# A fused DeltaNet and MLP kernel: the order of all its steps replaced by another, and its filler products given two widths

## The chip, the cores and the metric

The kernel runs on one core of a Trainium2 chip. Its time is the device time of one execution in microseconds (us); for one core the slowest core is that core. The time before is the median of three runs.

## The reference

An attention block (DeltaNet, a recurrence with a matrix state per batch and head), then layer norm and a two-layer MLP with ReLU, added to the block's output.

```python
batch, n_heads, seq, head_dim = (4, 8, 768, 48)      # q, k, v, beta; d_model = 8 * 48 = 384
def _attn_ref(q, k, v, beta):
    k_n = k / (np.linalg.norm(k, axis=-1, keepdims=True) + 1e-06)
    state = np.zeros((B, H, D, D))
    for t in range(S):
        y[:, :, t] = einsum('bhd,bhde->bhe', q[:, :, t], state)
        v_old = einsum('bhde,bhd->bhe', state, kt)
        state = state + bt * einsum('bhd,bhe->bhde', kt, vt - v_old)
def _moe_ref(x, g_ln, w_ch1, w_ch2):                  # w_ch1 384 x 1536, w_ch2 1536 x 384, in float64
    xn = (x - mu) / np.sqrt(var + 1e-06) * g_ln
    return x + np.maximum(xn @ w_ch1, 0.0) @ w_ch2
```

## The kernel before

The sequence of 768 tokens is cut into 12 chunks of 64. For each chunk c all 32 pairs of batch and head are worked on together: 64 tokens of two batches fill the 128 partitions. All arithmetic is float32; TensorE runs each float32 matmul call as two passes, each with a weight load of its own (a transpose is one pass).

For a chunk the attention part multiplies keys with keys (`gram`, G, L819) and queries with keys (`queries`, P, L819), inverts a triangular 64 x 64 matrix for each head, and carries the state on. For chunk 0 the inverse is made by products on TensorE, E1, Z1 to E5, Z5 (`first_inverse`, L770 and L786), with transposes and masked copies on VectorE and copies on ScalarE between them. For all others `rows_inverse` (L865) stores the products to DRAM, loads them back so that each head lies in one partition, eliminates 32 x 32 blocks on VectorE (pairs of instructions at L907 and L914, each waiting for the one before), and sends the result back by DRAM; `join` (L965) puts two blocks together with two products, e and z (L981, L987; for chunk 1 also L944 and L949). `recur` (L1021) then runs ks and qs (L1033), u (L1052, L1069 or L1088), s, the update of the state (L1105), and y, the output (L1095). Each of these is 32 matmul calls on tiles of 48 or 64 rows, 64 passes.

After y comes the layer norm on VectorE and ScalarE and the turn of its result to columns: by TensorE for chunks 0 to 2 (L1183), else by a store and four loads through DRAM (`xld`, `xnj`, DMA issued by SyncE). The MLP of chunk c (`mlp`, L1388) follows: for chunk 0 L1406 and L1448, for chunks 1 and 2 L1426 and `seven` (L1502), from chunk 3 on `fifteen` (L1274) and `seven`. `fifteen` replaces 18 block products of the first layer by 15 with sums on GpSimd (`mix`, L1290), VectorE (L1330) and ScalarE (L1325, L1334); its products are L1307, each step four passes of 128 columns over a bank of PSUM. `seven` does the second layer with 7 products in place of 8 (L1523, two passes of 192 columns a step; sums on GpSimd at L1510 and L1548, on VectorE at L1541). The weights come as 64-bit words (`fetch`, L568, DMA issued by ScalarE) and are converted by ScalarE, VectorE and GpSimd (`convert`, L579).

Every operation is a step: `Line.add` (L69) notes its engine, what it reads and writes, and a number, 0 to 3031, in the order in which the program names them. A step can hold many instructions (the 32 calls of a product), and the cost and due time given to it play no part in what follows. `ORDER` (L156 to L254) is a list of these numbers, with ranges; `Line.emit` (L101) goes through it and emits each step. `in_this_order` (L25) ties each instruction to the one before it on its engine, so the list sets the order on every engine, and the order of the DMA issues across SyncE and ScalarE. An engine that waits for a step's inputs holds up everything behind it in its queue.

The list also has the letter `f` three times. There `emit` takes the bank of the next TensorE step, asserts that nothing unread lies in it, and calls `idle` (L1597), which issues a matmul of 128 columns of the identity into that bank; its result is overwritten unread.

Of the kernel before, what the change touches and what calls it, by code (L numbers as in the profile page):

```python
# [53 lines left out]
class Line:  # L54
# [46 lines left out]
    def emit(self, tc):  # L101
# [7 lines left out]
        order = []  # L109
        for w in ORDER.split():  # L110
            a, b = (0, -1) if w == "f" else map(int, (w.split("-") * 2)[:2])
            order += self.steps[a : b + 1] or [None]
        nxt = None
        for n in range(len(order) - 1, -1, -1):
            if order[n] is None:
                order[n] = nxt.out
            elif order[n].eng == "PE":
                nxt = order[n]
        live = {}
        for s in order:  # L120
            if isinstance(s, tuple):
                assert not live.get(s[:2]), s
                self.filler(s)
                continue
# [5 lines left out]
            n = len(made)  # L130
# [26 lines left out]
52-53 51 54 65 10 9 57-58 55 320 56 306 398 67 319 63 62 66 308 249 654 7 64 8 61 11-12 2 33 14 25 24 71-72 68 0 15-16 34 21 27 13  # L157
1 26 18 31 19 3 75-76 82 6 17 83 70 77 73 84 36 99 37 97 74 38 101-104 93 100 78 69 79 30 28 80 20 85-86 81 110-111 87-88 116-117
113 205 105-106 f 39 120 107-108 119 121 94 114 206-207 115 208 90 92 91 46 656 42 44 43 40 59-60 45 41 109 251 258 112 122 118
124-125 123 132 134 133 126 128 22-23 127 140 138 135 89 137 136 131 129-130 141-143 139 146 230 98 144-145 218 149 152-154 160  # L160
147-148 156 155 150 157 96 95 151 158 32 161 168 159 219 169 29 170 162-164 176 174 255 405 252 256 402 253 257 254 307 305 401
318 395 317 220 214 232 171 173 165-166 172 216 212 167 240 242 209 47 657 4 177 175 184-186 231 178 192 179-180 210 183 238 187
181-182 188-189 236 190 221 233 48 658 49-50 193-195 201 241 191 243 197 259 202 235 204 362 203 198 200 199 361 309 311 234 196 f
310 331 260-262 35 248 250 263 211 237 264-265 213 239 332 312 222 329-330 333 335 355 313 334 314-315 226 5 266-269 215 270-273
223 274-276 337 277-279 321 323 322 324-325 338 280-289 336 224 356 326 341 327 342 290-295 343 217 653 225 666 659 655 353-354
426-427 f 347 244 429 428 245 349 339 348 350 227 340 344-346 430 567 569 431 568 228 246 571 432 351 316 406 328 397 393 296 404
403 396 467 352 229 247 665 668 461 660 357 572 575 570 363 573 576 407 303 298 300 297 301 299 304 302 469 468 466 399-400 394
579 593 574 359 580 577-578 594 583 408 465 584 581 587 599 582 600 588 368 365 358 364 360 409-410 667 411 605 585 591 366 412
367 470 586 589 413 379 590 592 380 606 611 595 597 661 369 371 596 601 471-474 477 476 414 478 475 415 370 372 434 670 392 672
671 669 391 416 374 373 598 603 612 604 417 419 418 385 433 609 420-421 610 386 424 375 383 602 425 422-423 381 630-632 615-616  # L170
435-436 782-783 785 787 917 784 786 789 788 780 920 916 617 607 479-504 376 505-508 387 437 382 388 509 377 438 673 439-440 378
608 384 389 442 441 443 445 390 618-619 613 633 662 620 634 1068 1080 677 1070 1072 1074 1067 444 614 446 790 450 447-448 510-515
451 516 449 517-520 452 521-539 663 674-675 924 664 676 923 779 679-680 678 681 926 635-636 621-622 637 623-624 638-640 457 453
625-626 641 540 642 645 627 646 644 919 928 544 541 543 542 460 459 456 458 455 791 454 794 825 682 826 647 683-686 689 792 823
831 821 832 837 822 827 781 688 690 1069 845 463 1082 1073 464 1071 838 843 828 833-834 691-696 651 697-698 545-546 687 652
699-700 556 648 701-702 649 703 839 547 549 548 550-551 553 824 552 840 554-555 844 793 829 795 830 796 835 797 800 836 802 848
922 1081 846 1079 1084 851 847 852 849 557 798 930 925 628 929 927 643 931 1173 1179 1181 629 918 1183-1184 1362 921 1182 1178
704-705 1075 706-708 805-806 841 854-858 799 558-560 801 810 709 803 1172 1185 1180 861 650 859 842 561 850 1085 1083 462 862 853
1086 863 1541-1542 811 710 804 812 711-713 807 860 808 714 932-933 864-866 871 867-869 817 934 562 870 820 564 563 566 715-716 809
717-721 936 722-726 872 889 881-882 813 565 814 818 816 873-874 883-885 890 875 886 891 876 727 877 1087 815 819 935 937 892-894  # L180
938 878 880 879 939 972 1186 887-888 895 1544 1554 1556 1543 940 1076 973 907 1077 978 908-910 896-899 979 984 900 911-912 901 941
# [76 lines left out]
def kernel(  # L258
# [13 lines left out]
    nc = tc.nc  # L272
# [61 lines left out]
    ident = sb("ident", [128, 128])  # L334
# [1262 lines left out]
    def idle(key):  # L1597

        nc.tensor.matmul(banks_of[key[:2]][:, 0:128], ident, ident[:, 0:1].to_broadcast([128, 128]))
# [152 lines left out]
```

## Time and profile before

| | |
|---|---|
| median of three runs | 520.41 us (519.92 to 522.11) |
| the profiled execution: its time | 520.78 us |
| its span, first to last instruction | 519.1 us |
| mean TensorE clock in it | 0.982 |
| DMA | 54.56 MB in 181,635 packets, 105 GB/s |

The difference between the profiled execution's time and its span, 1.7 us, lies outside the instructions. How rows are read: in a timeline a row is start, duration, engine, line, operation, output and inputs, shape and how many instructions, and in brackets how long the engine was idle before it and what ended that. PE is TensorE's matmul, PEld its weight load, counted apart. DVE is VectorE, ACT ScalarE, POOL GpSimd, SP SyncE. "issue" stands for a wait that ended for no reason that the profile shows. A row of a table of windows is the stretch, its length, the busy time and instruction count of each engine (PE, PEld, DVE, ACT, POOL, unless fewer are named), the granted TensorE clock as a share of full speed, the busy share of the 16 DMA engines and GB/s. In the lists of DMA queues stand packets, MB and the share of the 16 engines' time.

### The profile page before, as it was taken

To read this page: it belongs to the slowest core of one execution; us is meant where nothing else is said; L and a number is where in the kernel's file an instruction comes from. 1 tells how busy PE (TensorE), PEld (TensorE's weight loads), DVE (VectorE), ACT (ScalarE), POOL (GpSimd) and SP (SyncE) were. 2 spreads that over 40 slices of the span, in tenths; PEclk is the share of its full clock that TensorE was granted. 3 is DMA by queue.
4 is the path that set the end of the run, shared out by engine and by line. 5 is a ranking of instruction groups with operands and counts; after the bars stand their busy time and mean duration, and the time that the engine had idled before them with its cause. 6 is when DMAs were issued, how large, how long until landed. Compare 5 with 4: busy or idle time off the path is not lost.

```text
span 519.1 us, 22785 instructions
## 1 busy us (share of the span) xinstructions
PE 487.1 (94%) x9972; PEld 448.9 (86%) x9972; DVE 360.8 (70%) x814; ACT 206.9 (40%) x462; POOL 280.3 (54%) x447
## 2 busy tenths in 40 slices
PE   5577888999899999999999999999999999999997
PEld 4466786768798889999999989999999999999996
DVE  6577739798887567988889986757988446244241
ACT  5587845423431333234242632533513514424130
POOL 3435654604554877976764274473453742564554
PEclk9878998999999999999999999999999999999999
DMA  9957876585515866345853356643404403003011
GB/s 135 294 115 204 191 154 178 107 195 95 90 26 141 156 134 109 68 88 141 167 120 55 83 108 157 132 81 66 102 10 111 104 17 93 4 1 100 2 39 30
DMA packets 181635, 54.56 MB, mean 105 GB/s; under 512 B 164888, under 2 KB 177312, under 8 KB 181536
## 3 DMA queue, kind: packets, MB, share of 16 engines
q1 hardware_dynamic: 168512, 40.10, 37.9%
q10 hardware_dynamic: 10816, 9.83, 6.6%
q0 software_dynamic: 2208, 3.17, 3.8%
q8 instruction: 78, 1.28, 1.0%
q14 instruction: 21, 0.17, 0.1%
HBM read 36.30 MB, written 16.78 MB: 102 GB/s over the span
## 4 chain that ended last, share of the span: by engine, by line
PE 79%; DMA 5%; SPq 3%; issue 3%; DVE 3%; ACT 3%; POOL 2%; ACTq 0%; DVEq 0%; POOLq 0%
PE f L1523 27%; PE f L1307 22%; PE f L1426 6%; PE f L1448 3%; SPq L410 3%; PE two L819 3%; PE by L1033 2%; PE two L1033 2%; PE by L1095 2%; DMA xnt<-xld 2%; PE two L1088 2%; PE f L1406 1%; PE two L1105 1%; DMA words<-in_moe_w_ch_dram 1%; DMA gb<-gd 1%
## 5 line engine op out<-in xcount | busy, mean ns | idle before, releaser
L1510 POOL TENSOR_TENSOR h_all<-h_all 128x256 f32<-128x256 f32 x99 | 72.7, 745 | 30.5 <-PE f L1523 13.8
L1523 PE MATMUL f<-w_sb,h_all 128*128 128x192 f32 x396 | 82.2, 331 | 1.0 <-ACT h_all L1334 0.6
L1523 PE MATMUL f<-words,h_all 128*128 128x192 f32 x396 | 76.7, 329 | 0.0
L1523 PEld LDWEIGHTS f<-w_sb,h_all 128*128 128x128 f32 x396 | 65.1, 190 | 3.0 <-ACT h_all L1334 1.6
L1330 DVE TENSOR_TENSOR h_all<-f,h_all 128x512 f32<-128x512 f32 x72 | 48.9, 685 | 26.4 <-PE f L1307 19.3
L1523 PEld LDWEIGHTS f<-words,h_all 128*128 128x128 f32 x396 | 65.0, 190 | 1.5 <-issue 0.5
L1548 POOL TENSOR_TENSOR words<-h_all 128x128 f32<-128x128 f32 x66 | 31.2, 491 | 63.4 <-ACT h_all L1334 30.4
L907 DVE TENSOR_TENSOR tmp<-xb,gb 128x31 f32<-128x31 f32 (+19 forms) x139 | 57.5, 413 | 3.9 <-POOL xb L894 0.3
L1325 ACT COPY h_all<-f 128x512 f32<-128x512 f32 x45 | 26.2, 586 | 82.4 <-PE f L1307 68.8
L914 DVE TENSOR_TENSOR xb<-xb,tmp 128x31 f32<-128x31 f32 (+19 forms) x139 | 52.6, 378 | 3.7
L410 POOL DMA_DIRECT2D tb<-in_k_dram x64 | 42.2, 662 | 0.3 <-POOL tb L1630 0.3
L1334 ACT ACTIVATE h_all<-h_all 128x512 f32<-128x512 f32 x54 | 32.7, 626 | 23.9 <-DVE h_all L1330 23.5
L1307 PE MATMUL f<-x_new,w_sb 128*128 128x128 f32 x288 | 40.3, 278 | 0.1
L1307 PE MATMUL f<-xnt,w_sb 128*128 128x128 f32 x288 | 40.2, 277 | 0.0
L1307 PEld LDWEIGHTS f<-x_new,w_sb 128*128 128x128 f32 x288 | 36.5, 191 | 0.6 <-issue 0.2
L1307 PEld LDWEIGHTS f<-xnt,w_sb 128*128 128x128 f32 x288 | 36.5, 192 | 0.6 <-issue 0.2
L1541 DVE TENSOR_TENSOR o<-f,x 128x192 f32<-128x192 f32 x33 | 11.4, 352 | 36.8 <-PE f L1523 30.9
L1426 PE MATMUL f<-xnt,w_sb 128*128 128x256 f32 x144 | 34.5, 387 | 1.4 <-issue 1.4
L1426 PEld LDWEIGHTS f<-xnt,w_sb 128*128 128x128 f32 x144 | 26.4, 190 | 5.4 <-issue 1.8
L1523 PE MATMUL f<-w_sb,words 128*128 128x192 f32 x132 | 26.3, 329 | 0.0
L682 POOL TENSOR_TENSOR v<-v,kpair 128x768 f32<-128x768 f32 x10 | 14.7, 1473 | 14.0 <-DVE pt L897 14.0
L610 POOL TENSOR_TENSOR w_sb<-words 128x768 uint32<-128x768 uint32 (+1 forms) x11 | 14.7, 1348 | 13.7 <-ACT words L600 10.2
(239 smaller groups left out, 983.4 us busy)
## 6 DMA issues: line engine op xcount, KB each, us to landing
words<-in_moe_w_ch_dram ACTq DMA_DIRECT2D x20, 384.0 KB, 4.5
gd<-gsb SPq DMA_DIRECT2D x11, 512.0 KB, 3.9
v<-in_v_dram SPq DMA_DIRECT2D x24, 192.0 KB, 4.2
kr<-in_k_dram SPq DMA_DIRECT2D x46, 96.0 KB, 3.4
out_dram<-o SPq DMA_DIRECT2D x46, 96.0 KB, 2.2
xld<-xlt SPq DMA_DIRECT2D x9, 384.0 KB, 2.4
xnt<-xld SPq DMA_DIRECT2D x36, 96.0 KB, 2.9
tb<-in_q_dram SPq DMA_DIRECT2D x40, 64.0 KB, 2.8
```

The source lines that it names most:

```text
L410: add(eng, cost, lambda: QUEUE[eng].dma_start(out=out_, in_=in_), r, w, bulk=n * ns / 16e3, np=n, **kw)
L907: lambda j=j, n=n, w=w, t=t: nc.vector.tensor_tensor(out=t, in0=xv[:, 0:n, j : j + 1].to_broadcast([128, n, w]), in1=gv[:, j : j + 1, j + ...
L914: "DVE", dve(n * w), lambda t=t, rest=rest: nc.vector.tensor_tensor(out=rest, in0=rest, in1=t, op=ALU.subtract),
L1033: nc.tensor.matmul(dst[half(e), hp, j], src[drows(hp), (e if n else key_half(c, hp, e)) * GP + j], s_all[drows(hp), e, j], start=(n == 0 o ...
L1307: nc.tensor.matmul(wide(p[:, f : f + 128]), w[:, f : f + 128], r, start=start and i == 0, stop=True, skip_group_check=True)
L1325: add("ACT", act(512), lambda: nc.scalar.copy(o, p), pk, ok)
L1330: add("DVE", dve(512), lambda: nc.vector.tensor_tensor(out=o, in0=x, in1=y, op=op), [*xk_, *yk], ok)
L1334: add("ACT", act(512), lambda: nc.scalar.activation(o, o, ACTF.Relu, scale=scale), [], ok)
L1426: nc.tensor.matmul(p[:, 0:TOK], w1_sb[:, t, f * 128 : (f + 1) * 128], xnt[:, t], start=(t == 0), stop=(t == KC - 1))
L1510: add(eng, cost, lambda: e.tensor_tensor(out=out_, in0=x, in1=y, op=op), r, w, port=2 if eng == "Pool" else 1, pr=-2)
L1523: lambda f=f, t=start and f == order[0]: nc.tensor.matmul(p[:, 0:D2], lhs(f), rhs[:, f], start=t, stop=(f == order[-1]), skip_group_check=True
L1548: lambda f=f + i: e.tensor_tensor(out=s3[f], in0=one(0, 0)[0](f), in1=one(1, 0)[0](f), op=ALU.subtract),
```

## The change

The list `ORDER` is replaced whole. It names the same 3,032 steps, each once. Of the 954 steps of TensorE, 151 stand at the same place among TensorE's steps in both lists; the stages follow each other in the same manner (inverse of chunk 0, recurrences with MLP products between them, the MLP of chunks 10 and 11 alone at the end). The words that come with the change say that the plan behind the new list lets the transfer of a TensorE block wait until other transfers have run dry; of that plan the code holds only the list.

The fillers are now two: one `f`, among the first products of chunk 0, and one `F`, ahead of step 334, the second half of y0. `F` is a matmul of 512 columns in place of 128. The new `f` stands before the product of keys of chunk 1 (step 105). In the old list the three `f` stand before the second E1 (step 122), before a turn of chunk 2's keys (step 310) and before a turn of chunk 0's layer norm (step 347).

```diff
@@ -108,19 +108,19 @@
         for w in ORDER.split():
-            a, b = (0, -1) if w == "f" else map(int, (w.split("-") * 2)[:2])
-            order += self.steps[a : b + 1] or [None]
+            a, b = (0, -1) if w in "fF" else map(int, (w.split("-") * 2)[:2])
+            order += self.steps[a : b + 1] or [w]
         nxt = None
         for n in range(len(order) - 1, -1, -1):
-            if order[n] is None:
-                order[n] = nxt.out
+            if isinstance(order[n], str):
+                order[n] = (order[n], nxt.out[:2])
             elif order[n].eng == "PE":
                 nxt = order[n]
         live = {}
         for s in order:
             if isinstance(s, tuple):
-                assert not live.get(s[:2]), s
-                self.filler(s)
+                assert not live.get(s[1]), s
+                self.filler(*s)
                 continue
...
 ORDER = """
-52-53 51 54 65 10 9 57-58 55 320 56 306 398 67 319 63 62 66 308 249 654 7 64 8 61 11-12 2 33 14 25 24 71-72 68 0 15-16 34 21 27 13
...
-113 205 105-106 f 39 120 107-108 119 121 94 114 206-207 115 208 90 92 91 46 656 42 44 43 40 59-60 45 41 109 251 258 112 122 118
...
-181-182 188-189 236 190 221 233 48 658 49-50 193-195 201 241 191 243 197 259 202 235 204 362 203 198 200 199 361 309 311 234 196 f
...
-426-427 f 347 244 429 428 245 349 339 348 350 227 340 344-346 430 567 569 431 568 228 246 571 432 351 316 406 328 397 393 296 404
...
-922 1081 846 1079 1084 851 847 852 849 557 798 930 925 628 929 927 643 931 1173 1179 1181 629 918 1183-1184 1362 921 1182 1178
...
+51 53-54 52 65 9 57-58 56 55 308 63 319 398 62 306 67 66 320 7 64 10 249 11-12 2 15 14 22 13 18 0 42 8 61 40 46 654 44 41 43 60 59
+656 47 72 71 1 75-77 82 3 101-102 27 83 16 24 73 84 99 68 103 74 36 104 100 93 37 f 94 38 105-106 85 17 28 86 69 87 21 70 6 88 78
...
+204 200 199 198 202 211 241 237 310 329 239 263 35 196 243 250 264 331 227 330 333 332 F 334 234-235 214 312 335 361 356 355 336
...
+835 797 855-856 800 836 844 801 798 929 652 701 930 1176 931 643-644 1179 1181 628 1182 1172 1171 921 1183 918 629 1178 1180
+1184-1185 556 802 702-704 1075 841 857-859 799 932 557 922 842 805 705 806 706-709 803-804 849-850 852 851 1085 463 864-868 860
...
 """
...
@@ -1594,9 +1593,10 @@
-    def idle(key):
-
-        nc.tensor.matmul(banks_of[key[:2]][:, 0:128], ident, ident[:, 0:1].to_broadcast([128, 128]))
+    def idle(size, key):
+
+        n = 512 if size == "F" else 128
+        nc.tensor.matmul(banks_of[key][:, 0:n], ident, ident[:, 0:1].to_broadcast([128, n]))
 
     line.filler = idle
```

The diff is cut: of the list only the first lines, those with fillers, and those around step 557 (e of chunk 3) and step 798 (s of chunk 2) are shown. In the old list TensorE runs 800 (y of chunk 2), 557, 798 and then MLP steps; in the new one 800, 798, four MLP steps, P of chunk 3 (step 932) and then 557.

More of the change, by code (lines that the diff above doesn't have):

```diff
@@ L169 @@
[L169 to L172, printed above, removed]
@@ new lines @@
+2664 2661 2643 2640 2654 2646 2645 2655-2656 2662 2665 2674-2675 2663 2682-2685 2666 2742 2667-2668 2676 2671-2672 2677 2686
+2678-2679 2669 2687 2743 2574-2575 2680-2681 2573 2766 2673 2689 2688 2700-2702 2690-2694 2767 2703 2670 2770 2744-2746 2748-2749
+2768 2704-2705 2753 2777 2773 2809 2695-2696 2774 2769 2754-2755 2697 2771 2781-2782 2775 2783 2747 2772 2706 2750 2785-2786
+2778-2779 2751-2752 2756-2757 2819 2800 2787-2788 2814 2801 2784 2776 2780 2790-2791 2789 2794-2795 2797-2798 2796 2799 2802 2805
@@ new lines @@
+2886 2934 2917 2920-2922 2927 2930 2928-2929 2935-2936 2938-2939 2937 2940-2941 2952 2942 2887 2947 2931 2923-2924 2953-2954 2932
+2943-2944 2948 2925 2955-2958 2945-2946 2980 2959-2960 2970-2973 2981 2949 2926 2889 2713 2897 2888 2898 2982-2983 2964 2961-2962
+2967 2963 2968 2978 2977 2950 2974-2976 2951 2984-2988 2965 2989 3005 2997 3006 2998-2999 2990-2992 3000 2966 2969 2979 3001-3002
+3007-3009 3003-3004 2996 2994 3010 3012-3017 3011 2993 3018 2995 3023-3028 3019-3020 3029 3021 3030 3022 3031
```

171 lines of the change are left out of this document (83 added, 88 removed).

## Prediction

> **What bounds the kernel now.** I read the page first, then three stretches of the span, then what TensorE waited for.
>
> ```profile
> span 519.1 us, 22785 instructions
> PE 487.1 (94%) x9972; PEld 448.9 (86%) x9972; DVE 360.8 (70%) x814; ACT 206.9 (40%) x462; POOL 280.3 (54%) x447
> ```
>
> ```profile
> 0.00:104.00 104.00, 80.58 (x2348) 67.80 (x2349) 70.96 (x195) 64.74 (x149) 51.38 (x74) 0.92 0.78 173
> 104.00:500.00 396.00, 391.31 (x7529) 366.21 (x7528) 285.33 (x611) 139.30 (x309) 218.36 (x356) 1.00 0.44 91
> 500.00:519.10 19.10, 15.21 (x98) 14.91 (x97) 4.53 (x10) 2.89 (x6) 10.57 (x18) 0.96 0.08 21
> ```
>
> The first figure after each length is TensorE's busy time. It idles 23.4 us in the first 104 us, 4.7 us in the next 396, and 3.9 us behind its last product. An order can win only from these 32 us, from slow passes, and from the clock (0.92 in the first stretch). The waits name what is to be had:
>
> ```profile
> PE by L628 <- DVE kr L423: 6.1, 1, 6.1
> PE by L628 <- issue: 2.5, 1, 2.5
> PE f L987 <- issue: 1.7, 1, 1.7
> PE f L1426 <- issue: 1.4, 1, 1.4
> PE two L770 <- issue: 0.9, 2, 0.6
> PE f L1307 <- DVE h_all L1330: 0.8, 1, 0.8
> PE f L1523 <- ACT h_all L1334: 0.6, 1, 0.6
> PE two L1088 <- issue: 0.6, 1, 0.6
> PE f L786 <- issue: 0.5, 1, 0.5
> PE f L981 <- issue: 0.4, 2, 0.2
> PE f L1523 <- issue: 0.3, 1, 0.3
> ```
>
> The first 6.1 us is the arrival of the first keys; both orders begin with the same loads. The rows with "issue" sum to 8.3 us: waits for nothing that an engine or a data transfer explains. The timeline of TensorE around one shows what they are:
>
> ```profile
> 135.35 0.71 PE L981 MATMUL f<-xnj,gsb 32*32 32x32 f32 x59 [0.23 <-issue]
> 135.99 0.94 PE L1105 MATMUL two<-u,kr 64*48 64x48 f32 x64
> 136.85 1.35 PE L1426 MATMUL f<-xnt,w_sb 128*128 128x256 f32 x5
> 139.63 0.48 PE L1426 MATMUL f<-xnt,w_sb 128*128 128x256 f32 x1 [1.43 <-issue]
> ```
>
> Between the two stalls run 59 + 64 + 5 = 128 passes, and the second stall falls inside a product, five passes into six. The page has a queue for instructions:
>
> ```profile
> q8 instruction: 78, 1.28, 1.0%
> ```
>
> In the transfers of 135.3 to 137.1 us it has no packet, and this is the largest row:
>
> ```profile
> q1 hardware_dynamic: 1451, 0.17, 68.3%
> ```
>
> In 137.1 to 138.2 us it has one:
>
> ```profile
> q8 instruction: 1, 0.02, 5.2%
> ```
>
> 1.28 MB in 78 packets is 16.4 KB each, and 9,972 matmuls with 9,972 weight loads over 78 packets are 256 instructions each, 128 passes. So TensorE's program comes in blocks of 128 passes. The packet waits while data takes 68% of the transfer engines' time, moves when that is over, and TensorE resumes 1.4 us or more behind it, 4.28 us after the block began. A block that lasts less than its successor's transfer leaves TensorE standing. How long one lasts is set by what is in it:
>
> ```profile
> 114.64 10.56 PE f L1426 x48
> 474.42 11.63 PE f L1523 x70
> 489.79 11.32 PE f L1307 x100
> ```
>
> ```profile
> 372.80 0.61 PE L1307 MATMUL f<-x_new,w_sb 128*128 128x128 f32 x4
> 373.34 1.15 PE L1033 MATMUL by<-s_all,qt 48*64 48x48 f32 x64
> 374.31 1.11 PE L1088 MATMUL two<-v,xt 64*64 64x48 f32 x64
> ...
> 377.18 0.94 PE L1105 MATMUL two<-u,kr 64*48 64x48 f32 x64
> 377.93 0.28 PE L1095 MATMUL by<-u,pt 64*64 64x48 f32 x6
> ```
>
> 128 MLP passes take 14 to 28 us (128 x 11.32/100, 128 x 10.56/48), but 64 attention passes take about 1 us (373.34 to 374.31). Two attention products back to back use up a block in 2 us.
>
> **The change, part by part.** No product, copy or load is added or dropped, so all busy times stay except through the order, the clock and the fillers. I counted both orders step by step, 4 instructions for each matmul call (2 for a transpose), and gave every TensorE step the lower quartile of its own times from start to next start in this trace (0.447 us for four L1307 passes, 0.325 for two of L1523, 1.0 to 1.1 for 64 attention passes).
>
> *Blocks after 104 us (from block 18 on).* Before, seven of 59 blocks hold under 3.0 us of work (shortest 1.8, 2.3 and 2.6); in the new order none does. The work missing against a transfer of 3.0 us sums to 2.6 us before and 0 after; against 3.5 us, 6.8 and 1.5; against 4.0 us, 13.3 and 8.7; against 4.5 us, 22.9 and 20.7. The stalls there sum to some 2.6 us (1.4 + 0.6 + 0.3 + about 0.3), so the old shortfall matches a transfer near 3.0 us with some far later ones. I take -2.5 us. Bounds: -2.9, all of that and what the modelled ends of matmuls may hide, to +1.0, if the many new blocks of 3.1 to 3.8 us meet full queues.
>
> [...]
>
> *Blocks before 104 us.* There the sums hardly differ (3.5 us: 2.4 and 2.3). Two long stalls (L628 2.5 us, L987 1.7 us) each end a block that becomes longer, by 0.4 us (3.6 to 4.0) and 0.6 (2.9 to 3.5); two others become shorter (3.8 to 3.2, 4.4 to 3.1). I take -1.0. Bounds: -4.2, both long stalls gone, to +1.1, the two shortened blocks late by what they lost against 3.7 us.
>
> *Switches.* Four L1307 passes take 0.453 us in a row (11.32/25) and 0.54 when attention follows (372.80 to 373.34): 0.09. 64 L1105 passes take 0.75 us before attention (377.18 to 377.93) and 0.86 before an MLP product (135.99 to 136.85): 0.11. The old order changes between the kinds 140 times, the new one 126: 14 x 0.10 = -1.4 us. Bounds -1.4 to 0.
>
> *Fillers.* Two of 128 columns go, one of 512 comes. Two passes of 512 columns cost about 4 x 10.56/48 = 0.88 us. It stands before the second y0 product, at the place where TensorE now waits 0.7 us for the first:
>
> ```profile
> 48.05 0.68 PE L1095 MATMUL two<-u,pt 64*64 64x48 f32 x32 [0.69 <-DVE u L1074]
> ```
>
> Covered by that wait it costs nothing; without it 0.9, less the two small ones (0.25 each). I take 0; bounds -0.5 to +0.4.
>
> *Waits for data.* After 104 us those on TensorE sum to about 1.4 us (h_all rows above). In the list, 298 steps of TensorE after that point have their last producer less than 1 us of TensorE work ahead of them; in the new one 301. As tight as before: 0, bounds -1.4 to +1.4. SP's order moves one load far: a key load of chunk 4 (step 1174) goes from SP's 108th place to its 66th. It waits for s1, the last reader of its buffer; behind it stand the value loads of chunk 2 and the store of G4. In the new list s1 stands two products before G4, so the store is not ready earlier: 0.
>
> Sum, against the profiled execution's own 520.78 us: 520.8 - 2.5 - 1.0 - 1.4 = 515.9. That execution is 0.4 above the median of 520.41, so the median comes to **515.5**.
>
> **The rivals.**
>
> *Crossings are hidden anyway; the plan's spacing buys nothing.* The old stalls then come from chance meetings with full queues, and the new order meets as many. For: at 4.5 us per transfer the two orders differ by only 2.2 of 22.9 us, and some transfers took that long (4.28 above). Against: the shortest blocks are gone. Left are the switches: 520.4 - 1.4 = 519.0. [...]
>
> *The clock is won back too.* TensorE's clock over four stretches (busy, clock, DMA share):
>
> ```profile
> 12.33:22.57 10.24, 6.66 (x280) 1.00 1.16 266
> 22.57:32.81 10.24, 7.28 (x198) 0.50 0.71 199
> 87.43:90.84 3.41, 3.41 (x7) 0.50 0.04 12
> ```
>
> ```profile
> 28.91 1.13 PE L770 MATMUL by<-qt,gsb 64*64 64x64 f32 x32 [1.19 <-DVE qt L735]
> 33.21 0.69 PE L770 MATMUL by<-qt,gsb 64*64 64x64 f32 x32 [0.27 <-DVE qt L735]
> ```
>
> Half clock follows the 2.5 us stall and lasts 10.24 us; a product of 0.69 us takes 1.13 there, and about eight stand in it: 3.5 us. The second stretch costs half of its 3.41 us. If shorter stalls keep the clock up, 5.2 us more: 515.5 - 5.2 = 510.3. Against: the stretch ahead was only 6.66 us busy, mostly through waits on VectorE, which the change does not take away.
>
> *VectorE becomes the bound* (the slower side).
>
> ```profile
> 208.00:260.00 52.00, 51.13 (x894) 48.87 (x893) 46.38 (x92) 17.24 (x32) 38.47 (x59) 1.00 0.55 116
> 260.00:312.00 52.00, 51.28 (x1235) 48.14 (x1222) 46.47 (x97) 21.32 (x45) 27.72 (x49) 1.00 0.45 95
> ```
>
> The third busy figure is VectorE, 89% in these 104 us, spare 5.5 us in each 52. Its queue runs in order: the long chain of the block inverse (L907, L914) shares it with the sums (L1330) that free TensorE's banks. At three points of equal TensorE work (240, 270, 315 us) the new order has 1.5, 3.9 and 2.2 us more VectorE work ahead. Where the spare time lies behind the clump, TensorE waits these out: 7.6 us. Point of decision: a clump larger than the spare time before it. 520.4 - 3.9 + 7.6 = 524.1. Against: those waits are 0.8 us in all now, and elsewhere the new order has less VectorE work ahead, by up to 9.2 us.
>
> **How the numbers follow.** The forecast has 0.48, hidden crossings 0.21, the clock 0.13, VectorE 0.18. A measurement of this kernel tells about 0.5% (2.6 us) from no change, so faster is below 517.8 and slower above 523.0. Faster: 0.48 less 0.03 for its upper edge, plus 0.13 and 0.02 of hidden crossings, 0.60. Same: 0.22. Slower: 0.18. The likeliest case alone ranges from 512.5 to 518. For 8 in 10 the range goes from 510.0, the clock case taken in, to 523.5, just short of the VectorE case; all bounds at once would give 510.0 (520.4 - 2.9 - 4.2 - 1.4 - 0.5 - 1.4) to 524.3 (520.4 + 1.0 + 1.1 + 0.4 + 1.4).
>
> **What would show it.** Right: after 104 us the "issue" waits of TensorE fall below 1 us, their longest below 0.7; the switch rows keep their price. The first 104 us hold TensorE's idle time at 21 to 23.4 us. Wrong: "issue" rows of over 1 us in the middle of products after 104 us (crossings), a PEclk of 1.00 from 22 to 33 us (clock), or waits on DVE h_all above 3 us (VectorE). What would break it altogether is a start in which a weight piece lands late and a whole chain on ScalarE stands behind it, which no count of blocks shows.

## The result, and the profile after

The new kernel takes 517.25 us (median of 14 runs, 512.13 to 521.09), the old one beside it 521.16 us (14 runs, 519.34 to 524.27): ratio 0.9899, 95% interval 0.9865 to 0.9932. The ratio compares the means of the runs, a slow one of the new kernel (521.09 us) left out: 516.2 against 521.5 us. The prediction was 515.5 us against 520.41, a ratio of 0.9906. The execution profiled below took 517.98 us. In the new kernel's code every line behind the list has a number one lower than before.

The page of the new kernel, the head and the line of TensorE:

```profile
span 516.2 us, 22793 instructions
PE 484.4 (94%) x9970; PEld 448.6 (87%) x9970; DVE 360.4 (70%) x814; ACT 206.5 (40%) x462; POOL 280.4 (54%) x447
```

The same three stretches as before (length, busy time of PE, PEld, DVE, ACT and POOL with instructions, then granted clock, DMA share, GB/s):

```profile
0.00:104.00 104.00, 79.42 (x2240) 66.35 (x2244) 70.43 (x191) 62.66 (x145) 45.62 (x68) 0.92 0.75 164
104.00:500.00 396.00, 392.64 (x7668) 370.26 (x7661) 287.25 (x618) 142.85 (x315) 225.67 (x366) 1.00 0.45 94
500.00:516.20 16.20, 12.38 (x78) 12.03 (x76) 2.74 (x7) 0.97 (x3) 9.07 (x15) 0.97 0.09 24
```

TensorE idles 24.6 us in the first 104 us (before 23.4), 3.4 in the next 396 (before 4.7). By 104 us it has run 2240 passes and the old kernel 2348, but the orders differ and so do the passes in them; a fair comparison needs equal work (below). What TensorE waited for, over the whole span (total, times, longest), the rows that matter:

```profile
PE by L627 <- POOL ident L430: 6.3, 1, 6.3
PE by L1094 <- issue: 2.4, 1, 2.4
PE f L785 <- issue: 2.0, 2, 1.1
PE f L980 <- issue: 1.8, 1, 1.8
...
PE two L1087 <- issue: 0.8, 1, 0.8
...
PE f L986 <- issue: 0.6, 2, 0.4
PE f L1306 <- DVE h_all L1329: 0.6, 1, 0.6
PE two L769 <- issue: 0.5, 1, 0.5
```

The old "issue" rows of 2.5 us (L628) and 1.7 us (L987) in the start and of 1.4 us (L1426) in the middle are gone, but others of 2.4, 2.0 (two waits) and 1.8 us stand in the start. Only L1087 and L986, 1.4 us together, lie behind 104 us.

To see where the gain arises, the two executions are cut at a product that both orders run after the same work. The first attention product of x1 (step 546, 64 passes of 32x32) is one: ahead of it both have done the same TensorE work, but for one attention product that the new order runs just before it and the old one later. In the old kernel's timeline, that product and the last ones of the span:

```profile
125.13 0.75 PE L981 MATMUL f<-xnj,gsb 32*32 32x32 f32 x64
...
513.10 2.11 PE L1523 MATMUL f<-w_sb,h_all 128*128 128x192 f32 x12
```

And in the new kernel's:

```profile
127.14 1.15 PE L1032 MATMUL two<-s_all,kt 48*64 48x48 f32 x64
128.22 0.75 PE L980 MATMUL f<-xnj,gsb 32*32 32x32 f32 x64
...
510.26 2.11 PE L1522 MATMUL f<-w_sb,h_all 128*128 128x192 f32 x12
```

Old: 513.10 + 2.11 - 125.13 = 390.1 us from this point to TensorE's end. New: 510.26 + 2.11 - 128.22 = 384.2, and 1.1 (127.14 to 128.22) for the product already done: 385.2. The later part is 4.9 us quicker; up to the cut the new kernel is 2.0 us slower (128.22 against 125.13 + 1.08). These two numbers, called *rest* and *arrival* below (both put to equal work), are what the experiments look at, for the later part repeats more closely than the start.

### The profile page after: what moved, and what is told of

Same layout as the page of the kernel before. It is cut to its first block, busy times and chain, and to the rows that moved or that the text cites. A ratio compares the mean times of both kernels' runs of the same rounds, so it can differ in the third digit from the quotient of the medians.

```text
span 516.2 us, 22793 instructions
## 1 busy us (share of the span) xinstructions
PE 484.4 (94%) x9970; PEld 448.6 (87%) x9970; DVE 360.4 (70%) x814; ACT 206.5 (40%) x462; POOL 280.4 (54%) x447
## 4 chain that ended last, share of the span: by engine, by line
PE 80%; DVE 6%; DMA 5%; issue 3%; SPq 2%; ACT 2%; POOL 0%; ACTq 0%; DVEq 0%; POOLq 0%
PE f L1522 27%; PE f L1306 21%; PE f L1425 6%; PE two L818 4%; PE f L1405 3%; PE f L1447 3%; SPq L409 2%; PE by L1032 2%; PE by L1094 2%; PE two L1032 2%; PE two L1104 2%; PE two L1087 2%; DMA gb<-gd 2%; DMA gd<-gsb 1%; PE f L627 1%
## 5 line engine op out<-in xcount | busy, mean ns | idle before, releaser
L1509 POOL TENSOR_TENSOR h_all<-h_all 128x256 f32<-128x256 f32 x99 | 72.0, 740 | 21.5 <-DVE tmp L906 10.2
L1522 PE MATMUL f<-w_sb,h_all 128*128 128x192 f32 x396 | 80.0, 329 | 0.0
L1522 PE MATMUL f<-words,h_all 128*128 128x192 f32 x396 | 78.5, 330 | 0.0
L1522 PEld LDWEIGHTS f<-w_sb,h_all 128*128 128x128 f32 x396 | 65.3, 190 | 1.4 <-ACT h_all L1434 0.2
L1522 PEld LDWEIGHTS f<-words,h_all 128*128 128x128 f32 x396 | 65.0, 190 | 0.9 <-issue 0.2
L1547 POOL TENSOR_TENSOR words<-h_all 128x128 f32<-128x128 f32 x66 | 29.4, 468 | 46.8 <-ACT h_all L1333 23.2
L906 DVE TENSOR_TENSOR tmp<-xb,gb 128x31 f32<-128x31 f32 (+19 forms) x139 | 49.7, 357 | 3.9 <-POOL xb L893 0.3
L1306 PE MATMUL f<-x_new,w_sb 128*128 128x128 f32 x288 | 39.6, 276 | 0.0
L1306 PE MATMUL f<-xnt,w_sb 128*128 128x128 f32 x288 | 39.0, 277 | 0.6 <-DVE h_all L1329 0.6
L1306 PEld LDWEIGHTS f<-x_new,w_sb 128*128 128x128 f32 x288 | 36.7, 192 | 0.1
L1306 PEld LDWEIGHTS f<-xnt,w_sb 128*128 128x128 f32 x288 | 35.8, 192 | 0.9 <-POOL ident L1289 0.7
L1522 PE MATMUL f<-w_sb,words 128*128 128x192 f32 x132 | 26.2, 332 | 0.0
L1132 ACT COPY x<-by 128x384 f32<-128x384 f32 x23 | 10.4, 479 | 36.4 <-PE by L1094 22.6
```

Of the source, the lines that this page charges most:

```text
L906: lambda j=j, n=n, w=w, t=t: nc.vector.tensor_tensor(out=t, in0=xv[:, 0:n, j : j + 1].to_broadcast([128, n, w]), in1=gv[:, j : j + 1, j + ...
L1306: nc.tensor.matmul(wide(p[:, f : f + 128]), w[:, f : f + 128], r, start=start and i == 0, stop=True, skip_group_check=True)
L1509: add(eng, cost, lambda: e.tensor_tensor(out=out_, in0=x, in1=y, op=op), r, w, port=2 if eng == "Pool" else 1, pr=-2)
L1522: lambda f=f, t=start and f == order[0]: nc.tensor.matmul(p[:, 0:D2], lhs(f), rhs[:, f], start=t, stop=(f == order[-1]), skip_group_check=True
L1547: lambda f=f + i: e.tensor_tensor(out=s3[f], in0=one(0, 0)[0](f), in1=one(1, 0)[0](f), op=ALU.subtract),
```

## The experiments

All runs but the one with added passes, each beside the old kernel on the same chip. Arrival and rest in us, from the one profiled execution of each:

| kernel | median | ratio to old, 95% | arrival | rest |
|---|---|---|---|---|
| old | 521.16 | 1 | 126.2 | 390.1 |
| old again | 522.78 (one run) | | 129.5 | 388.8 |
| new | 517.25 | 0.9899, 0.9865 to 0.9932 | 128.2 | 385.2 |
| new again | 516.45 | 0.9877, 0.9830 to 0.9923 | 127.5 | 385.4 |
| old start, new rest | 517.96 | 0.9888, 0.9853 to 0.9924 | 129.1 | 385.2 |
| new start, old rest | 525.03 | 1.0061, 1.0028 to 1.0093 | 128.9 | 389.9 |
| new, blocks shifted by 80 instructions | 531.12 | 1.0172, 1.0132 to 1.0212 | 129.4 | 397.4 |
| new, shifted by 256 | 518.15 | 0.9895, 0.9858 to 0.9931 | 131.2 | 384.4 |
| old, shifted by 56 | 534.51 | 1.0239, 1.0187 to 1.0291 | 131.8 | 398.2 |
| new, its large filler small | 518.94 | 0.9930, 0.9898 to 0.9962 | 130.3 | 383.7 |
| new, no fillers | 520.11 | 0.9958, 0.9921 to 0.9995 | 133.3 | 385.4 |
| new, fillers in the start | 519.69 | 0.9944, 0.9918 to 0.9970 | 129.9 | 384.8 |

**Old start, new rest, and its mirror image.** The list is cut where both orders have done the same TensorE work, and the other order's list, without the steps already done, follows. Old start (three of its lines, the second one where the lists meet):

```diff
 ORDER = """
-51 53-54 52 65 9 57-58 56 55 308 63 319 398 62 306 67 66 320 7 64 10 249 11-12 2 15 14 22 13 18 0 42 8 61 40 46 654 44 41 43 60 59
+52-53 51 54 65 10 9 57-58 55 320 56 306 398 67 319 63 62 66 308 249 654 7 64 8 61 11-12 2 33 14 25 24 71-72 68 0 15-16 34 21 27 13
...
+579 593 574 359 580 365 465 358 360 364 594 583 599 584 367 661 410 587 577 588 368 578 591 581 592 582 366 408-409 600 411 470
...
```

> The old order up to the 413th step (m0's first product on the fourth bank behind G4, at 65.6 us before and 72.0 us after; both prefixes hold the same 39.35 us of TensorE work), the new order for all that is left; the old list's third filler is left out so that the instruction blocks of the rest lie as in the new list. Between this point and the end the profiled execution of the new kernel was 9.3 us quicker than the old one's (6.4 us behind at the cut, 2.9 ahead at the end). Theory: the new plan wins in the later blocks and loses part of it in its start; then this kernel takes 520.8 - 9.3 = 511.5 us, within 2 us. Rival (the late start of the new kernel is an accident of one execution, and its median already holds the whole gain): 517, as the new kernel.

New start (against the new kernel):

```diff
 ORDER = """
 51 53-54 52 65 9 57-58 56 55 308 63 319 398 62 306 67 66 320 7 64 10 249 11-12 2 15 14 22 13 18 0 42 8 61 40 46 654 44 41 43 60 59
...
-359 465 668 358 360 364 580 594 583 599 584 574 367 661 410 587 577 588 368 578 591 581 592 582 366 408-409 600 411 470 585 379
+359 665 668 461 574 580 577-578 594 583 408 465 584 581 587 599 582 600 588 368 358 364 360 409-410 667 411 605 585 591 366 412
...
```

> The mirror image: the new order up to its 409th step, the old one for the rest. Theory: the start costs what the profiled execution shows, up to 6.4 us, and nothing is won back: 524 to 527 us. Rival (accident): 521, as the old kernel. Rival (the gain sits in the start): below 519.

The rest follows the list it comes from: 385.2 with the new one, 389.9 with the old one (385.2 and 390.1 in the kernels themselves; in all profiles below at the lists' own boundaries 383.7 to 385.4 and 388.8 to 390.1). That half of the theory holds. The other half falls: with the old start the kernel takes as long as the new one (0.9888 against 0.9899), not 511.5 us, and its start, the same list that arrived at 126.2 us in the old kernel, arrived at 129.1. The 6.4 us that the theory read out of one pair of executions are not to be had: in part they were chance (the old start reached the meeting point at 70.1 us here, at 65.6 in the old kernel), and what is left is given back behind that point, as the repeats below show. The mirror image is 0.6% slower than the old kernel, the lower end of what was expected; whether that is the start or the seam stays open.

**The block boundaries, moved and nothing else.** Tiny matmuls ahead of the first product, in a wait of 6.3 us, push all later boundaries (step 0, which writes the `eps` that they read, goes ahead of them):

```diff
-            a, b = (0, -1) if w in "fF" else map(int, (w.split("-") * 2)[:2])
+            a, b = (0, -1) if w in "fFt" else map(int, (w.split("-") * 2)[:2])
...
+0 t t t t t t t t t t t t t t t t t t t t 51 53-54 52 65 9 57-58 56 55 308 63 319 398 62 306 67 66 320 7 64 10 249 11-12 2 15 14
...
+        if size == "t":
+            nc.tensor.matmul(banks_of[key][0:1, 0:16], eps, eps.to_broadcast([128, 16]))
+            return
```

> The new order, unchanged, with 20 tiny matmuls (one weight column, 16 data columns) ahead of its first product, in the 6.3 us in which TensorE has nothing yet: they push every later boundary of TensorE's instruction blocks by 80 instructions (40 passes). Theory (blocks): from 87 us of TensorE work on, the work missing against a transfer of 3.0 us rises from 0 to 8.1 us, against 3.5 us from 1.5 to 15.7; the kernel takes 8 to 14 us longer, 525 to 531, with 'issue' stalls at the new boundaries. Rival (crossings hidden, the gain is the switches'): 517, within 1.5.

As the control the same with 64 of them, one whole block:

> The counterpart of the run with 20 tiny matmuls: 64 of them, 256 instructions, one whole block, so that every later boundary falls where it did in the new kernel (their 128 passes of 31 ns take 4 us of the first 6). Theory (it is the place of the boundaries that costs): 517, within 2 us. Rival (tiny matmuls ahead of the start do harm by themselves, through the start or the clock): 531 or more.

And on the old order, 14 of them:

> The old order with 14 tiny matmuls ahead of its first product: every boundary 56 instructions (28 passes) earlier in the work. The work missing behind 87 us of TensorE work rises from 2.6 to 7.3 us against 3.0 us, from 6.8 to 12.6 against 3.5 us. Theory (blocks): the kernel takes 4.7 to 6 us longer than the old one, ratio 1.009 to 1.013. Rival (only the new order is laid out for its boundaries, the old one lies by chance): within 2 us of the old one.

Shifted by 80 instructions, the same order with the same products takes 531.1 us; shifted by a whole block, 518.2. The rest grows by 12.2 us (385.2 to 397.4) in the one and shrinks by 0.8 in the other. This is the place of the boundaries and nothing else, and it is the largest effect in this study. The shift is near the worst there is: counted as in the prediction, the work missing behind 87 us against 3.0 us lies between 0 and 9.3 us for the new order, by where the boundaries fall, and is 8.5 at this shift. TensorE's waits from 126 to 500 us in the kernel shifted by 80:

```profile
PE f L987 <- issue: 2.8, 3, 1.9
PE two L819 <- issue: 2.6, 2, 1.4
PE by L1095 <- issue: 1.9, 1, 1.9
...
PE by L987 <- issue: 0.6, 1, 0.6
PE f L1523 <- issue: 0.4, 1, 0.4
```

"issue" sums to 8.3 us there (1.4 in the new kernel). One of the stalls, in that kernel's timeline, and then three windows around it (the first figure after the length is TensorE's busy time, the third from the end its granted clock, the second from the end the DMA share):

```profile
147.83 1.15 PE L1033 MATMUL two<-s_all,kt 48*64 48x48 f32 x64
148.91 0.74 PE L987 MATMUL f<-xt,es 32*32 32x32 f32 x62
151.58 0.31 PE L987 MATMUL f<-xt,es 32*32 32x32 f32 x2 [1.94 <-issue]
151.82 1.01 PE L1523 MATMUL f<-w_sb,h_all 128*128 128x192 f32 x2
```

```profile
148.20:151.60 3.40, 1.46 (x118) 1.29 (x109) 3.37 (x5) 0.00 (x0) 3.31 (x5) 1.00 0.23 35
151.60:155.00 3.40, 3.40 (x14) 3.25 (x15) 0.26 (x1) 1.58 (x6) 0.12 (x1) 0.50 0.02 5
155.00:158.40 3.40, 3.40 (x58) 3.17 (x60) 1.69 (x5) 1.51 (x6) 0.00 (x0) 1.00 0.00 0
```

Two attention products stand behind each other, 62 of the second's 64 passes run, and TensorE stands for 1.94 us inside a product, with the transfer engines at 0.23: data takes little of them. In the 3.4 us behind it the clock is halved (0.50): two passes of L1523 take 0.8 us (151.82 to 152.62, the start of what follows) where two otherwise take 0.325. So this stall was paid twice. A second such pair stands at 206 to 213 us; the two half-clock stretches cost up to 1.7 us each (half of 3.4), which with the 6.9 us of added stalls makes most of the 12.2 (a wait of 1.4 us of L1307 on VectorE is new there too).

The old order shifted by 56 shows the same: the old order too depends on where its boundaries lie, and its own place is a good one (2.7 us missing against 3.0 us, of 2.2 to 7.5 by the shift; 7.3 at 56). Whether that is plan or luck no run shows. Its rest grows by 8.1 to 9.4 us (388.8 and 390.1 to 398.2). Here the expected size was missed (ratio 1.009 to 1.013, measured 1.0239): the "issue" waits behind 126 us grew to 7.0 us (from about 2.5), as the missing work said, but two half-clock stretches of 6.8 and 3.4 us follow the stalls of 2.4 and 2.2 us, and the arrival is 2 to 6 us later, which was in no count.

**The cost of a boundary by itself.** 640 passes in the shape of an attention product, five blocks, are added at two places:

```diff
+        if size == "q":
+            for i in range(32):
+                e, h = i % 2, i // 2 % 2
+                nc.tensor.matmul(
+                    by[half(e), h, 0:48], w1_sb[half(e ^ h), 0, half(e)], w1_sb[half(e ^ h), 0, 128:176]
+                )
+            return
...
+412 586 605 597 589 606 369 590 374 598 371 q q q q q q q q q q 413 380 611 603 595 434 471-474 477 476 478-480 370 481 414 482
...
+2892-2894 2869 2903 2870 2895 2904 2879-2884 2902 2910 2871 2914 2905 2896 q q q q q q q q q q 2911-2912 2885 2907-2909 2913
```

> The cost of a boundary measured by itself: the new order with 640 passes added at each of two places, in the shape of an attention product (64 passes of 64x48 in about 1.0 us, each quadrant in turn): ahead of step 413 (80 us in the profile of the new kernel, data uses 0.7 of the transfer engines) and ahead of step 2911 (487 us, data uses 0.01). 640 passes are five blocks, so all other boundaries stay where they are. Rival (crossings hidden): 10 us at each place, the kernel 20 us longer. Theory: a block of 2.0 us of work is not long enough for its successor's transfer, so the five blocks take as long as five transfers: 3.0 us each at the quiet place, 15 us in all; 3.5 to 4.5 each at the busy one, 17 to 22 us; the kernel 32 to 37 us longer.

The kernel took 550.8 us, 33.5 more than the new one. The quiet place, in TensorE's timeline (L1602 is the added matmul), and all that the transfer engines moved in 500 to 522 us:

```profile
503.34 3.70 PE L1602 MATMUL by<-w_sb 64*64 64x48 f32 x237
508.02 2.08 PE L1602 MATMUL by<-w_sb 64*64 64x48 f32 x128 [0.97 <-issue]
511.49 2.08 PE L1602 MATMUL by<-w_sb 64*64 64x48 f32 x128 [1.39 <-issue]
515.23 2.08 PE L1602 MATMUL by<-w_sb 64*64 64x48 f32 x128 [1.67 <-issue]
518.98 0.55 PE L1602 MATMUL by<-w_sb 64*64 64x48 f32 x19 [1.67 <-issue]
```

```profile
q8 instruction: 5, 0.08, 1.6%
q14 instruction: 1, 0.01, 0.1%
```

Each stall comes after exactly 128 passes, with nothing but instructions being moved. From start to start a block takes 3.47, 3.74 and 3.75 us, though its work takes 2.08. The first one was quicker: the boundary inside the 237 passes lies 109 passes behind their start, at 504.9 us, and the next at 508.02, 3.1 us on. So with idle transfer engines the first short block behind long ones took 3.1 us here, short blocks in a row up to 3.75. The busy place:

```profile
79.26 2.77 PE L1602 MATMUL by<-w_sb 64*64 64x48 f32 x173
84.66 3.08 PE L1602 MATMUL by<-w_sb 64*64 64x48 f32 x128 [2.63 <-issue]
88.66 5.81 PE L1602 MATMUL by<-w_sb 64*64 64x48 f32 x256 [0.92 <-issue]
96.12 1.48 PE L1602 MATMUL by<-w_sb 64*64 64x48 f32 x83 [1.65 <-issue]
```

The boundary ahead of the first stall lies 45 passes into the 173, at 79.94 us. The four blocks from there on, each with its length, busy times, granted clock, DMA share and GB/s:

```profile
79.94:84.66 4.72, 2.09 (x142) 1.97 (x134) 0.00 (x0) 1.08 (x2) 0.00 (x0) 1.00 0.74 198
84.66:88.66 4.00, 3.08 (x128) 2.93 (x128) 0.00 (x0) 0.00 (x0) 0.00 (x0) 0.59 0.16 26
88.66:92.39 3.73, 3.66 (x128) 3.50 (x128) 0.00 (x0) 0.00 (x0) 0.00 (x0) 0.52 0.02 4
92.39:96.12 3.73, 2.08 (x128) 1.96 (x128) 0.00 (x0) 0.00 (x0) 0.00 (x0) 1.00 0.02 4
```

Only the first block met the traffic that the place was chosen for, and it took 4.7 us where the first one of the quiet place took 3.1; its packet of instructions started 2.3 us behind the boundary, against 0.8 to 1.2 us at the first four boundaries of the quiet place. While TensorE stood, the transfers ran dry (0.74, 0.16, then 0.02 of the engines), so the last two blocks are no test beside data, and the third was bound by its own work at half clock (3.66 of 3.73 us). The theory holds on the whole: 3.0 us each was right for the first block of the quiet place and too low for those behind it, and the one block beside data took a little more than the 3.5 to 4.5 us expected. It is a single block, so the size of that surcharge is open.

**The fillers.** The 512-column filler of the new kernel in TensorE's timeline, ahead of the second y0 product:

```profile
45.27 1.10 PE L1094 MATMUL two<-u,pt 64*64 64x48 f32 x32
46.30 1.73 PE L1599 MATMUL by<-ident 128*128 128x512 f32 x2
47.97 0.44 PE L1094 MATMUL by<-u,pt 64*64 64x48 f32 x15
50.80 0.58 PE L1094 MATMUL by<-u,pt 64*64 64x48 f32 x17 [2.40 <-issue]
```

Made small, then both fillers taken out:

```diff
-204 200 199 198 202 211 241 237 310 329 239 263 35 196 243 250 264 331 227 330 333 332 F 334 234-235 214 312 335 361 356 355 336
+204 200 199 198 202 211 241 237 310 329 239 263 35 196 243 250 264 331 227 330 333 332 f 334 234-235 214 312 335 361 356 355 336
```

> The new order with its one filler of 512 columns made one of 128 (same number of instructions, so the same blocks). In the profiled execution its two passes took 1.73 us, two of 128 columns took 0.4 there. Theory: it is on the path, and the kernel gains about 1.3 us: 516. Rival 1 (it stands in a wait): 517.2, no change. Rival 2 (it keeps the clock up): a longer stretch at half clock from 44 us on, 2 us or more slower.

```diff
-656 47 72 71 1 75-77 82 3 101-102 27 83 16 24 73 84 99 68 103 74 36 104 100 93 37 f 94 38 105-106 85 17 28 86 69 87 21 70 6 88 78
+656 47 72 71 1 75-77 82 3 101-102 27 83 16 24 73 84 99 68 103 74 36 104 100 93 37 94 38 105-106 85 17 28 86 69 87 21 70 6 88 78 19
...
-204 200 199 198 202 211 241 237 310 329 239 263 35 196 243 250 264 331 227 330 333 332 F 334 234-235 214 312 335 361 356 355 336
+199 198 202 211 241 237 310 329 239 263 35 196 243 250 264 331 227 330 333 332 334 234-235 214 312 335 361 356 355 336 265-266 215
```

> The new order without its two fillers (8 instructions less ahead of all later boundaries; work missing against 3.0 and 3.5 us 0 and 0.9 us, 0 and 1.5 with them). Theory: the fillers win nothing, the kernel stays within 1.5 us of the new one (517), by the missing work 0.5 us below it. Rival (they keep the clock up): a longer stretch at half clock ahead of 60 us, 3 us or more slower.

Both theories missed. Made small, the filler wins nothing (0.9930 against 0.9877 to 0.9899 for the kernels with the large one, the intervals overlap). Without fillers the kernel takes 520.1 us, some 0.6 to 0.8% more than with them; these intervals only just overlap. The rest is that of the new order (385.4), so the loss lies ahead of the cut; how large it is there the arrival of 133.3 us doesn't tell, for it comes from an execution of 523.3 us, 3.2 above that kernel's median. The rival, the clock, has the granted clock of the single executions for it: its median is 0.970 in the twelve without fillers, 0.977 in the twelve with the small one, 0.985 and 0.990 in the fourteen and six of the new kernel (the old one beside the first two: 0.984 and 0.982). That the lower clock makes the whole loss isn't shown; the stalls of that start may have a part in it.

The opposite, 22 more small fillers at nine waits of the start and 40 tiny matmuls to make up one block (three of the new list's lines):

```diff
+121 108 97 119 f f f f 124-125 f f f f 132 25 112 134 122 90 137 135 218 205 113 230 115 133 140-141 f f f 143 123 34 109 251 258
...
+95 149 98 206 224 305 255 257 252 256 254 395 405 317 307 402 401 396 399 318 404 48 45 49 209 153 160-161 159 f f f 168 219 162
...
+202 211 241 237 310 f f 329 239 263 35 196 243 250 264 331 227 330 333 332 F 334 234-235 214 312 335 361 356 355 336 265-266 215
```

> A try at a better kernel: the new order with 22 more fillers of 128 columns at nine places of the first 45 us at which TensorE waits for another engine (4, 4, 3, 2, 3, 1, 1, 2 and 2 of them ahead of steps 124, 132, 143, 158, 168, 176, 192, 201 and 329), and 40 tiny matmuls ahead of the first product, 248 instructions in all, so that the later blocks stay within 8 instructions of where they are. If the half-clock stretches of the start follow windows in which TensorE was busy about half of the time, they become fewer, and the kernel takes 512 to 515. Rival (the waits are shorter than the fillers, or the extra block comes late): 518 to 522.

The clock did stay up, 1.00 over the first 52 us against 0.92 in the profile of the new kernel, and the kernel was no faster for it: 519.7 us (0.9944). In its timeline the eight passes of fillers ahead of step 124 take 2.07 us and the eight ahead of step 132 1.62, more than TensorE waited at these places in the new kernel (1.39 and 1.54 us):

```profile
15.37 2.07 PE L1603 MATMUL by<-ident 128*128 128x128 f32 x8
17.37 1.13 PE L770 MATMUL by<-qt,gsb 64*64 64x64 f32 x32
18.43 1.62 PE L1603 MATMUL f<-ident 128*128 128x128 f32 x8
```

Step 124's product begins at 17.37 here, at 14.6 and 15.8 in the two profiles of the new kernel.

**Both kernels again.** Unchanged, for a second profile each:

> The new kernel unchanged, on the same chip as these. The old start so far reached 39.35 us of TensorE work at 65.6 and 70.1 us, the new start at 70.3 to 72.3. Theory (the start differs by several us from one execution to the next through the clock; behind 87.8 us of work the new order is 4.9 us quicker in each): the time from 87.8 us of work to the last product is 394.1 us, within 1 us (394.1 and 394.1 so far with the new rest, 399.0 and 398.8 with the old). Rival (that part varies as much as the start): off by more than 2 us.

> The old kernel unchanged, profiled a second time. If its quick start (39.35 us of TensorE work done at 65.6 us) belongs to the old order, it comes again, within 2 us, and the new order's start is about 4 us dearer (70.3 to 72.8 in six profiles, 69.6 in one). If it was one execution's luck with the clock, it comes at 68 us or later, and the two starts cost about the same. Behind 87.8 us of work: 399.0 us to the last product, within 1 us, by either.

The times from 87.8 us of TensorE work to the end in these two texts (394.1, 399.0, 398.8) are all 6.2 us too large; added up rightly they were 387.9 twice with the new rest and 392.8 and 392.6 with the old one. The new kernel again: 388.0. The old one again: 391.5, 1.3 off, just outside. The old start's quick beginning came again (39.35 us of work done at 67.2 us; with the new start at 72.0 and 69.6), but it is given back: from there to 87.8 us of work the old order needs 56.8 and 58.5 us, the new one 52.4 and 54.2. By the cut the old arrives at 126.2, 129.5 and (with the new rest behind it) 129.1, the new at 128.2, 127.5 and (with the old rest) 128.9: means of 128.3 and 128.2, with up to 3.3 us between executions of one start.

No kernel tried beats the new one by more than the intervals allow; 0.9877, 0.9888, 0.9895 and 0.9899 are one time.

## Why the prediction was right, and where not

The time was right, 0.9899 measured and 0.9906 forecast, and so were the two mechanisms named first: the gain lies where the later blocks and the switches were said to bring it. The rest is 389.6 us with the old list at its own boundaries (mean of three) and 384.9 with the new one (mean of seven), a gain of 4.7; no gain is to be seen in the arrival. That the sum came out so well is luck in part: two terms brought about 1.8 us less than forecast, and 1.6 us that no term foresaw fill their place. By terms:

- *Blocks after 104 us, -2.5.* The mechanism is shown: moving the boundaries alone cost 12.2 us. Its share of the gain is smaller than forecast. Over the products that hold a boundary (time from start to next start, above the median of their kind) the excess is 6.5 us with the old list (6.45, 5.98, 6.97 in three profiles) and 4.8 with the new one (4.54, 5.29, 4.84, 3.78, 5.55 in five): -1.7, less by some tenths if a product at the edge of a boundary is put down the other way. It was mis-sized by reading the price as a fixed 3.0 us; the many blocks of 3.1 to 3.8 us that the new order makes can still pay when they follow each other (up to 3.75 us each in the probe) or meet data (4.7 in the probe; in the new kernel the block from 196.9 to 201.5 us took 4.6 beside a DMA share of 0.76 and ended in a stall), as the upper bound of that term had it. So the forecast that "issue" behind 104 us falls below 1 us failed: it is 1.4 us, and 0.9 to 2.0 in other profiles of the new rest, longest 1.0. One thing was left unsaid in the working: its blocks of 128 passes leave out TensorE's semaphore instructions. Five stalls inside products of the new kernel (24.0, 42.0, 50.8, 86.2 and 269.1 us) fall at one place modulo 256, to one instruction, only if TensorE's 132 semaphore instructions are counted with its matmuls and weight loads; in passes alone the place drifts from 91 to 67 modulo 128. Counted with them, the missing work against 3.0 us comes to 2.7 and 0 us, as forecast (2.6 and 0).
- *Switches, -1.4.* Right. Over eight profiles two L1522 passes take 0.325 us before their like and 0.418 before attention, four L1306 passes 0.447 and 0.540; a product of L1032 takes 0.969 before attention and 1.078 before MLP, one of L1104 0.755 and 0.865. Products of L818, L980 and L986 take the same before either, which the flat 0.10 left out. Summed by these medians behind the cut: 7.8 us with the old list, 6.5 with the new one, -1.3. All 14 switches that the new order saves lie there.
- *Blocks before 104 us, -1.0.* Not seen: the arrivals are equal (128.3 and 128.2), though three executions each, up to 3.3 us apart, could hide 1 us. In the profile the two long stalls that were to shrink did vanish, but the rows of 2.4 us (L1094), 1.8 (L980) and 2.0 (L785, two) took their place. The step looked at the blocks that grew, and too little at what the transfer engines do beside the others: the block that ends in the 2.4 us row took 8.8 us (42.0 to 50.8), with no packet of instructions until 48.1 and a DMA share of 0.83. TensorE's idle time in the first 104 us, forecast at 21 to 23.4, was 24.6 (23.7 in the second profile).
- *Fillers, 0.* The large one took 1.73 us at a clock of 0.50 (0.88 was reckoned, at full clock), yet making it small won nothing, and taking both out lost about 3 us. That the change of fillers costs nothing fits; a worth of some 3 us lies outside the bounds given, -0.5 to +0.4, which looked at the fillers' own time only.
- *Waits for data, 0.* Right as far as the rows go: those on DVE and ACT behind 104 us sum to 1.7 us in the new profile, 1.6 in the old one.
- *What is left.* -1.7 and -1.3 make 3.0 of the 4.7. The other 1.6 us (8.8 against 7.2, the excess of products that hold no boundary, over the same profiles) come in pieces of 0.1 to 0.4 us, most of them at the same product in each execution of a list. Their cause isn't settled.

*The rivals.* Crossings are not hidden: the order with its boundaries shifted by 80 instructions should then have taken what the one shifted by 256 takes, and is 13 us slower; the rival's 519.0 (0.9973 of the old time) lies above the interval too. The probe's blocks of 2.08 us of work, which took 3.1 to 4.7, speak against it too, though behind 104 us the new kernel shows an "issue" wait at three of some 58 crossings only. The clock was not won back, though the sign named for it came, a clock of 1.00 from 22 to 33 us: other stretches at half clock (16.8, 44.1 and 51.0 us) took the old one's place, and it is 0.92 over the first 104 us in both profiles. Over whole executions its median is 0.985 in the new kernel and 0.977 to 0.984 in three sets of runs of the old one. VectorE did not become the bound: L1306 waits 0.6 us for h_all. The runs of the new kernel at 512 to 515 us beside others at 516 to 521 do point to its start, where executions of one list differ by 3 us and more.

## What to carry to other kernels

Where TensorE's stalls end for no reason that an engine or a data transfer gives, count its instructions, its semaphore instructions with them. Here such stalls fell at one place modulo 256, to one instruction (five inside products of the new kernel), and short blocks of 2.08 us of work took 3.1 us with idle transfer engines, up to 3.75 where several followed each other, 4.7 in one block beside data. Where a count shows the same, a block of short passes should hold about as much work as such a block takes. Such an order is tied to its count: 80 instructions more ahead of it cost the rest 12.2 us here, 256 more and 8 fewer nothing (384.4 and 385.4 us against 385.2). So any edit that changes the number of TensorE instructions should be made up to a whole block, or the order planned anew. And one pair of profiles does not tell a start from another: a part that repeats within 1.7 us and one that scatters by 3 us should be measured apart.

## What the runs showed that was not expected

**The clock was halved for stretches of 3.41 us and multiples of it.** The start of the new kernel, cut into windows of that length, five stretches of one window each, the fourth of three (the third column counts TensorE's busy time, the clock is the third figure from the end):

```profile
40.73:44.15 3.42, 1.72 (x61) 1.24 (x57) 2.45 (x5) 3.29 (x9) 2.58 (x2) 1.00 0.61 91
44.15:47.56 3.41, 3.41 (x89) 2.56 (x79) 2.50 (x7) 1.26 (x3) 0.81 (x3) 0.50 0.93 235
47.56:50.98 3.42, 1.02 (x29) 0.50 (x30) 1.00 (x6) 0.00 (x0) 0.00 (x0) 1.00 0.99 298
50.98:61.22 10.24, 8.88 (x221) 7.82 (x216) 6.88 (x30) 6.30 (x12) 2.71 (x4) 0.50 0.50 159
61.22:64.63 3.41, 2.31 (x26) 2.01 (x19) 0.18 (x1) 2.82 (x7) 3.21 (x5) 1.00 0.46 142
```

A window busy for 1.72 of 3.42 us is followed by one at half clock, one busy for 1.02 by three; the window of 2.31 was followed by none. In the twelve profiles of the table the stretches at half clock, but for the one at TensorE's end, last 3.4, 6.8, 10.2, 13.7, 17.1 or 20.5 us. The limit is not sharp. All thirteen profiles, cut into such windows from their first clock figure on (10.0 us in the new kernel, 12.3 in the old), give 26 at full clock in which TensorE was busy for 0.50 or less, each followed by half clock; from 0.51 to 0.69 it was 15 of 70; above that none. So the stall of 1.94 us in the kernel shifted by 80, in 3.40 us of which TensorE was busy for 1.46, was followed by 3.4 us at a clock of 0.50, by estimate up to 1.7 us more.

**Some short blocks cost nothing.** In the kernel shifted by 80, two attention products make up the block from 271.8 to 273.5 us, 1.8 us long, beside a busy data queue (66% of the transfer engines' time), and no stall follows:

```profile
271.76 1.15 PE L1033 MATMUL two<-s_all,kt 48*64 48x48 f32 x64
272.84 0.75 PE L981 MATMUL by<-xnj,gsb 32*32 32x32 f32 x64
273.52 1.24 PE L1523 MATMUL f<-words,h_all 128*128 128x192 f32 x6
```

The queue of instructions moved two packets in the long block ahead of it (255.7 to 271.8 us) and none in the short one: what came next must have been there already. The same holds for the blocks of 2.0 us at 220.8 and 2.3 us at 288.8. So the prediction's rule, that a block shorter than its successor's transfer leaves TensorE standing, does not always hold, and a count of missing work can overstate the stalls. What lets a second packet come early was not tested.
